# Attention scores in 48 drained stays of one and a half fills, in place of 63 stays of four or seven heads

## The chip, the cores and the metric

The kernel runs on one core of one Trainium2 chip. The metric is the device time of one execution in microseconds (us); a kernel's figure is the median of its runs. TensorE (PE) multiplies matrices into PSUM, a memory of eight banks of 128 partitions x 512 fp32 values; ScalarE (ACT) and VectorE (DVE) read PSUM, GpSimd (POOL) works on SBUF alone, and SyncE (SP) issues transfers.

## The reference

A gated mix of two branches over one sequence of 2048 tokens of width 512, in bf16:

```python
g = _sigmoid((x * gate_w).sum(-1, keepdims=True))
a = _A_ref(x, A_wq, A_wk, A_wv, A_wo, A_beta)     # attention with a memory, 32 heads of 16
b = _B_ref(x, B_W_gate, B_W_up, B_W_down)         # relu(x Wg) * (x Wu) Wd, inner width 1792
return g * a + (1 - g) * b
```

Branch A cuts the sequence into four segments of 512 tokens. In a segment each head has causal softmax attention over the segment alone, and it recalls from a running memory of the segments before:

```python
logits = jnp.einsum('bhqd,bhkd->bhqk', qs, ks) * scale + mask
p = _softmax(logits, axis=-1)
a_dot = jnp.einsum('bhqk,bhkd->bhqd', p, vs)
num = jnp.einsum('bhld,bhde->bhle', pq, M)
den = jnp.einsum('bhld,bhd->bhl', pq, z)[..., None] + 1e-06
o = g * a_mem + (1.0 - g) * a_dot
```

The step that the change touches is the first of these: the scores q k^T and their exponentials.

## The kernel before

**Plan and order.** The body doesn't issue instructions as it goes. `plan.add` (line 144) makes a numbered task with its engine, a modelled duration, what it depends on, and the PSUM banks and ring buffers that it takes (`need`) and gives back (`frees`). `ORDER` (line 31) is a list, written out, of all 1362 task numbers; `UNITS` (line 97) names the bank or buffer of each slot. `Plan.run` walks the list, and the tasks are emitted in that order, so that each engine's queue is a subsequence of it. The durations in the tasks play no part in what is emitted.

**TensorE's three ways of work.** A full product (`full`, line 491) uses the array as one tile of 128 x 128 (line 493) or, where `Plan.run` has marked the stretch as a column stretch, as four column tiles of 128 x 32 that stream at the same time (line 497). The attention output P V (`pv`, line 757), the memory update (line 880) and the denominators (line 814) always use column tiles. The scores (`visit`, lines 673 to 716) use four row tiles of 32 x 128: row tile j holds head j of a group of four, since a head has 16 channels and two heads of a pair share 32 rows. So every visit to the scores is a change of the array's tiling on the way in and one on the way out. This text calls a visit a **stay**.

**Units and fills.** A unit u (16 of them, four to a segment) is a group of eight heads over one segment's 512 queries. Its scores come as four **fills** of 4 x 512 columns (row tile j fills one bank of 512), the causal pieces in `PIECES` packed so that each fill is full; the 64-wide diagonal pieces ("d") of two units together make a fifth fill in every second unit. That is 72 fills. `tape` strings their 4 x 72 items (unit, fill, row tile) together, and `SIZES` (line 987) cuts the tape into 63 stays: 51 of four items and 12 of seven. A stay of four takes four banks, each row tile one; a stay of seven takes seven, and lasts as long as two fills, since three of its row tiles do two items and one does one. One bank (`HOST`, line 988) then belongs to a tile of the down projection that is open across the stay (`hosts`).

**After the scores.** One ACT instruction (line 714) takes the exponential of up to four banks at once, from PSUM into a bf16 tile `E` (six of them, `RE`), or `Em` for the diagonal. POOL masks the diagonal blocks of `E` (line 730), DVE those of `Em` (line 738). `pv` multiplies with V; DVE normalises and transposes (lines 788 to 769). Between the stays, PE runs the projections of q, k, v, the gate and up products of branch B (`ffn_tasks`, line 915) and the down and output products (`out_tile`, line 942), whose results DVE and ACT move out of PSUM bank by bank.

Of the kernel before, what the change touches and what calls it, by code (L numbers as in the profile page):

```python
# [12 lines left out]
P = 128  # L13
# [12 lines left out]
RE = 6  # L26
# [68 lines left out]
"""  # L95

UNITS = (
    "530476210000046222023013110375010151700000200100000010110000010010300002100011030239202431"
    "38122a1100320531063217203d01220031013b102c010200022111230020111123201232201323103121342013"
    "000000000230010000023000000000130003000005010027c60293205511810373200120410212106326a012d1"  # L100
    "1132232204b0001020011712110631071222222010322117021132520310000000003200000000320010000002"
    "3000300003200162687116300c222a31340019020b302321156037102132427150110d01020002317312117110"
    "31131346511047603102000000000720100000013000000000230100000050103234617c0128512d1031321522"
    "0010190103301a6136504b4077322200120110020"
)


class Slot:


    def __init__(self, cands):
        self.cands, self.units, self.left = tuple(cands), (), 0

# [79 lines left out]
def kernel(  # L193
# [56 lines left out]
    hT = ring([P, L], BF16, "hT", RH)  # L250
    T = ring([P, 2, L], F32, "T", 1)
    ex1 = ring([P, L], BF16, "ex1", 3)
    ktr = ring([P, L], BF16, "ktr", 4)
    pkT = ring([P, L], BF16, "pkT", 4)
    rgr = ring([P, L], BF16, "rgr", 3)
    och = ring([P, L], BF16, "och", 2)
# [816 lines left out]
```

## Time and profile before

| What | us |
|---|---|
| three runs, median (range) | 262.33 (262.08 to 262.55) |
| the profiled execution: its time | 262.61 |
| its span in the trace | 260.9 |
| DVE busy | 202.1 (77%) |
| ACT busy | 183.0 (70%) |
| POOL busy | 67.3 (26%) |
| PE weight loads busy | 120.7 (46%) |

A row of a timeline gives the start and the length of some instructions of one line that follow each other, in us from the span's start, then the engine, the line, the operation, output and inputs, the shape (rows x columns of the array tile, then the output) and the count. PE is a matrix multiplication, PEld a weight load. The length of a matmul in the trace includes its way through the array, so that matmuls overlap; what a matmul costs is read from one start to the next. A row of a group of instructions ends with busy time, mean ns of one, and the engine's idle time before them with what ended it.

### The profile page before, as it was taken

How to read it: one execution, taken by the hardware profiler on the slowest of the kernel's cores; microseconds unless marked ns; L12 is line 12 of the kernel's file. 1: busy time of each engine (PE TensorE's matmuls, PEld its weight loads, DVE VectorE, ACT ScalarE, POOL GpSimd, SP SyncE). 2: the span in 40 equal slices, each digit the busy share in tenths (PEclk: the TensorE clock that was granted, in tenths of full speed). 3: DMA queues.
4: the chain of work that ended last, by engine and by line, in shares of the span. 5: the costliest groups of instructions: out<-in, count | busy, mean ns of one | idle time of the engine just before them, and what ended most of it. 6: DMA issues, size and time to landing. Idle time of an engine off the chain costs nothing.

```text
span 260.9 us, 9058 instructions
## 1 busy us (share of the span) xinstructions
PE 254.1 (97%) x3914; PEld 120.7 (46%) x3942; DVE 202.1 (77%) x452; ACT 183.0 (70%) x186; POOL 67.3 (26%) x188
## 2 busy tenths in 40 slices
PE   8999999999999999999999999999999999999995
PEld 3444444444545444454545444444545444445445
DVE  2499889999888957998998894697888736596622
ACT  3199899998889678797377837989477875793000
POOL 8018742224322213113021242124112422112000
PEclk9999999999999999999999999999999999999999
DMA  7999963030006243300016541000000043000011
GB/s 194 314 284 259 283 140 105 3 68 13 3 23 132 64 114 75 68 3 3 15 35 107 167 110 57 4 0 8 14 0 10 7 145 112 0 3 3 3 40 43
DMA packets 31600, 19.75 MB, mean 76 GB/s; under 512 B 16072, under 2 KB 30024, under 8 KB 31560
## 3 DMA queue, kind: packets, MB, share of 16 engines
q1 hardware_dynamic: 31144, 18.90, 28.6%
q8 instruction: 31, 0.51, 0.9%
q10 hardware_dynamic: 416, 0.26, 0.3%
q14 instruction: 9, 0.07, 0.1%
HBM read 13.21 MB, written 2.55 MB: 60 GB/s over the span
## 4 chain that ended last, share of the span: by engine, by line
PE 97%; issue 1%; DVE 0%
PE ps L493 53%; PE ps L497 25%; PE ps L685 9%; PE ps L757 7%; PE ps L1006 1%; PE ps L880 1%; PE ps L855 0%; PE ps L531 0%; PE ps L814 0%; DVE osr L961 0%; PE ps L540 0%
## 5 line engine op out<-in xcount | busy, mean ns | idle before, releaser
L714 ACT ACTIVATE E<-ps 128x2048 bf16<-128x2048 f32 (+3 forms) x79 | 120.4, 1552 | 26.4 <-PE ps L685 25.6
L730 POOL TENSOR_SCALAR_AFFINE_SELECT E<-E 128x256 bf16<-128x256 bf16 x128 | 53.7, 448 | 155.0 <-ACT E L714 149.1
L931 DVE TENSOR_TENSOR hT<-ps,rgr 128x512 bf16<-128x512 f32 x56 | 37.8, 681 | 21.9 <-PE ps L493 13.5
L925 ACT ACTIVATE rgr<-ps 128x512 bf16<-128x512 f32 x56 | 32.7, 596 | 20.3 <-PE ps L493 11.1
L493 PE MATMUL ps<-xT,wu_sb 128*128 128x512 bf16 x158 | 41.9, 380 | 0.6 <-issue 0.5
L493 PE MATMUL ps<-xT,wg_sb 128*128 128x512 bf16 x132 | 34.9, 379 | 0.6 <-issue 0.3
L493 PE MATMUL ps<-wd_sb,hT 128*128 128x512 bf16 (+2 forms) x147 | 29.5, 339 | 1.4 <-issue 1.3
L685 PE MATMUL ps<-QT,KT 32*128 32x64 bf16 (+3 forms) x768 | 27.8, 244 | 0.0
L788 DVE STREAM_TRANSPOSE T<-ps 128x512 f32<-128x512 f32 x32 | 21.9, 701 | 3.5 <-PE ps L757 3.1
L497 PE MATMUL ps<-wd_sb,hT 128*32 128x512 bf16 x384 | 24.0, 380 | 0.0
L493 PEld LDWEIGHTS <-wu_sb 128*128 128x128 bf16 x164 | 14.9, 98 | 18.5 <-issue 2.5
L497 PE MATMUL ps<-xT,wg_sb 128*32 128x512 bf16 x344 | 23.1, 380 | 0.0
L685 PEld LDWEIGHTS <-KT 32*128 32x128 bf16 x768 | 11.0, 92 | 24.1 <-issue 22.8
L961 DVE TENSOR_SCALAR osr<-ps,ngcol 128x512 bf16<-128x512 f32 (+2 forms) x18 | 12.2, 682 | 11.3 <-PE ps L493 10.4
L493 PEld LDWEIGHTS <-wg_sb 128*128 128x128 bf16 x138 | 12.9, 98 | 15.7 <-issue 1.3
L493 PEld LDWEIGHTS <-hT 128*128 128x128 bf16 x156 | 13.5, 98 | 14.1 <-issue 2.3
L757 PE MATMUL ps<-E,Vp 128*17 128x320 bf16 (+3 forms) x512 | 19.1, 273 | 0.0
L714 ACT ACTIVATE Em<-ps 128x2048 bf16<-128x2048 f32 (+2 forms) x11 | 15.6, 1415 | 4.3 <-PE ps L685 4.1
L497 PE MATMUL ps<-xT,wu_sb 128*32 128x512 bf16 x240 | 16.2, 379 | 0.0
L588 DVE CAST QT<-ps 128x512 bf16<-128x512 f32 x16 | 10.9, 684 | 6.0 <-PE ps L493 5.5
L493 PE MATMUL ps<-xT,wq_sb 128*128 128x512 bf16 x49 | 14.3, 407 | 0.2 <-issue 0.2
L493 PE MATMUL ps<-wv_sb,xT 128*128 128x512 bf16 x54 | 13.9, 379 | 0.4 <-issue 0.3
(100 smaller groups left out, 308.7 us busy)
## 6 DMA issues: line engine op xcount, KB each, us to landing
out_dram<-osr SPq DMA_DIRECT2D x15, 128.0 KB
xn<-in_A_x_dram SPq DMA_DIRECT2D x3, 512.0 KB
xn<-coefs SPq DMA_DIRECT2D x6, 256.0 KB
cdr<-coefs SPq DMA_DIRECT2D x6, 256.0 KB
wg_sb<-in_B_W_gate_dram SPq DMA_DIRECT2D x2, 512.0 KB
wu_sb<-in_B_W_up_dram SPq DMA_DIRECT2D x2, 512.0 KB
wd_sb<-in_B_W_down_dram SPq DMA_DIRECT2D x2, 512.0 KB
wg_sb<-in_B_W_gate_dram SPq DMA_DIRECT2D x2, 384.0 KB
```

The costliest lines, as they stand in the source:

```text
L493: nc.tensor.matmul(out, lhsT=lhsT, rhs=rhs, start=start, stop=stop)
L497: nc.tensor.matmul(out[r], lhsT=lhsT[:, r], rhs=rhs, start=start, stop=stop, tile_position=(0, 32 * j))
L588: prj["q", seg, c] = plan.add("DVE", 600, key - RQK, lambda: nc.vector.tensor_copy(QT[i][:], bank(sl)), [a] + war, DVL, frees=[sl])
L685: nc.tensor.matmul(ps[:, o:o + w], lhsT=lhsT.rearrange("p h q -> p (h q)"), rhs=rhs, start=True, stop=True, tile_position=(32 * j, 0))
L714: lambda n0=n0, n1=n1, u=u, f=f, j0=j0, j1=j1: nc.scalar.activation(target(u, f, j0, j1), ps[:, banks[n0] * L:(banks[n0] + n1 - n0) * L], ...
L730: nc.gpsimd.affine_select(out=m[:, :, o:o + HP], in_=m[:, :, o:o + HP], compare_op=ALU.is_ge, fill=0.0, base=HP, pattern=[[0, 4], [1, HP]] ...
L757: nc.tensor.matmul(bank(sl)[32 * m:32 * m + HW, q:q + w], lhsT=(Vp[i] if n < 4 else Vm)[:, kb, r, 4 * c + j, 0:HW], rhs=rhs, start=(n == 0 ...
L788: done.append(plan.add("DVE", 633, key - RL, lambda r=r, sl=sl: nc.vector.transpose(T[ts.i][:, r], bank(sl)), [a] + done, 75 if r else 0, ...
L880: nc.tensor.matmul(bank(sl)[32 * j:32 * j + 32, 34 * g:34 * g + 34], lhsT=pK[i][:, t, g * P + 32 * j:g * P + 32 * j + 32], rhs=Vp[i][:, t, ...
L925: r = plan.add("ACT", 478, key - RL, lambda sl=gsl, rs=rs: nc.scalar.activation(rgr[rs.i][:], bank(sl), ACT.Relu), [g], ACL, frees=[gsl])
L931: nc.vector.tensor_tensor(hT[hs1.i][:], bank(sl), rgr[rs.i][:], ALU.mult)),
L961: nc.vector.tensor_scalar(osr[os.i][:, n0 - c0:n1 - c0], bank(sl)[:, 0:n1 - n0], ngcol[:, tt:tt + 1], None, ALU.mult)),
```

## The change

The tape of items goes. Each unit has three stays (48 in all), and each does one whole fill and half of another: fill 0 with the first half of fill 1, fill 2 with the other half of fill 1, fill 3 with the unit's own half of the diagonal fill. A stay takes three pairs of banks: the whole fill has a bank for each row tile, as before, and the half fill puts row tiles 0 and 1 into one bank and 2 and 3 into another, 256 columns each. So that two row tiles never write one bank at the same time, the stay has two parts with `nc.tensor.drain()` between them: in the first, row tiles 0 and 2 write their half fill and 1 and 3 the first 256 columns of their whole fill; in the second come the other 512 columns of each row tile. Exponentials go by bank pair, 1024 columns an instruction, three for each stay. The score matmuls become 928 from 768, since pieces are cut at column 256.

With it: a seventh `E` tile, `ktr` and `pkT` rings of three for four; each of the two `pv` groups of a unit waits for the masks of its own two fills alone; the diagonal mask goes by unit; the down projection's tiles take any free bank; `ORDER` and `UNITS` are new lists of 1401 tasks and 635 slots.

```diff
-RE = 6
+RE = 7
 ORDER = """
...
-    ktr = ring([P, L], BF16, "ktr", 4)
-    pkT = ring([P, L], BF16, "pkT", 4)
+    ktr = ring([P, L], BF16, "ktr", 3)
+    pkT = ring([P, L], BF16, "pkT", 3)
...
+    def pieces(u, f, c0, c1):
+
         if f == "d":
+            for kb in range(4):
+                yield kb, 2, kb * P, HP, HP * kb
+            return
+        for kb, q, o in PIECES[f // 2]:
+            a, b = max(o, c0), min(o + L - q, c1)
+            if a < b:
+                yield kb, 3 * (f % 2), q + a - o, b - a, a
+
+    def parts(u):
+
+        return [((u, 0, None), (u, 1, 0)), ((u, 2, None), (u, 1, 1)), ((u, 3, None), (u, "d", u % 2))]
+
+    def visit(u, n, key):
+        whole, half = parts(u)[n]
+        pairs = [(0, 1), (2, 3), (4, 5), (6, 7), (1, 2), (3, 4), (5, 6)]
+        sls = [Slot([(("ps", a), ("ps", b)) for a, b in pairs[k:] + pairs[:k]]) for k in range(3)]
+        h0 = 0 if half[1] == "d" else half[2] * L // 2
+        mm = ([], [])
+        for j in range(4):
+            n = 0
+            for part, c0, c1, late in (((half, h0, h0 + L // 2, 0), (whole, 0, L, 1)),
+                                       ((whole, 0, L // 2, 0), (whole, L // 2, L, 1),
+                                        (half, h0, h0 + L // 2, 1)))[j % 2]:
+                for kb, o, q, w, at in pieces(*part[:2], c0, c1):
+                    base = (2, j * L // 2 + at - h0) if part is half else (j // 2, j % 2 * L + at)
+                    mm[late].append((n, j, base, kb, o, q, w))
+                    n += w + 6
 
         def pe():
...
+            for late in range(2):
+                if late:
+                    nc.tensor.drain()
+                for _, j, (k, at), kb, o, q, w in sorted(mm[late]):
+                    rows = slice(32 * j, 32 * j + 32)
+                    at += sls[k].i * L
+                    nc.tensor.matmul(ps[:, at:at + w],
+                                     lhsT=KT[u % RK][rows, kb, o:o + 2].rearrange("p h q -> p (h q)"),
+                                     rhs=QT[u % RQ][rows, q:q + w],
+                                     start=True, stop=True, tile_position=(32 * j, 0))
...
+            def ex(k=k, f=f, h=h, sl=sl):
+                src = ps[:, sl.i * L:(sl.i + 2) * L]
+                if f == "d":
+                    dst = Em[:, :, h].rearrange("p j k q -> p j (k q)")
+                else:
+                    dst = E[(NFILL * u + f) % RE].rearrange("p (j q) -> p j q", j=4)
+                    dst = dst[:, 2 * k:2 * k + 2] if h is None else dst[:, :, h * L // 2:(h + 1) * L // 2]
+                nc.scalar.activation(dst, src.rearrange("p (j q) -> p j q", j=2 if h is None else 4),
+                                     ACT.Exp, scale=SCALE)
...
-        while any((u, f) not in tape_done for f in FILLS(u)):
-            score()
+        for n in range(3):
+            visit(u, n, KA(u - LEAD, AUNIT * n / 3))
...
-            a = plan.add("PE", 550, key - PVP + r, pv, masks + [prj["v", seg, t] for t in range(4)]
+            a = plan.add("PE", 550, key - PVP + r, pv, masks[r::2] + more + [prj["v", seg, t] for t in range(4)]
...
-            eread[NFILL * u + f] = [a]
+            eread[NFILL * u + f] = [groups[f % 2][1]]
...
-            sl = plan.one("ps", [HOST] if tt < 12 else OBANKS if n0 < 3 * P else (5, 4))
+            sl = work() if tt < NT - 1 else plan.one("ps", OBANKS if n0 < 3 * P else (5, 4))
```

More of the change, by code (lines that the diff above doesn't have):

```diff
@@ L31 @@
 ORDER = """
[63 rows of a table removed]
[65 rows of a table added]
 """
 UNITS = (
[L98 to L104, printed above, removed]
+    "731620540000016010041027222153010120600100100134000001011001250010010010000100110000000016"
+    "70007129322c70335135412b40472232214120362134021a4208117d0010223170512031222032012100100231"
+    "22355330612465120302300100164000111044000030110000000000200030000040111000151150016025b110"
+    "8102a0110021d71130217300202347151405c32097112110250001010020050012212001115304121451712030"
+    "00444000050100000000001601100000000011010100000000021011401d1107100a1175001112020173021901"
+    "70120600147168021c001b02100110007201204001726236055011437203210000000005000100000044402000"
+    "0000000003100100000000050011310102100154120511485027020b1172021d01392003120a223c7176411062"
+    "11001"
 )
@@ L572, in proj_q @@
         old = u - RQ
-        war = [att.get(("score", old)), att.get(("score", old // 2 * 2, "d"))]
+        war = [att.get(("score", old))]
         pwar = [att.get(("recall", old)), att.get(("denpe", old // 4, old % 4 // 2))]
@@ L600, in proj_k @@
         old = u - RK
-        war = [att.get(("score", old)), att.get(("score", old // 2 * 2, "d"))]
+        war = [att.get(("score", old))]
         a = matmuls(key, [(w, 0.25) for w in war if w], sl, proj_mm(wk_sb, c, seg),
@@ L651 @@
     PIECES = [[(0, HP, 0), (3, 7 * HP, 7 * HP)], [(1, 3 * HP, 0), (2, 5 * HP, 5 * HP)]]
-    eread, exps = {}, {}
-    def item(u, f, j):
-        rows = slice(32 * j, 32 * j + 32)
+    eread, exps, stays = {}, {}, []
+    def pieces(u, f, c0, c1):
         if f == "d":
-            for v in range(2):
-                i = (u + v) % RQ
-                for kb in range(4):
-                    yield (KT[(u + v) % RK][rows, kb, 2:4], QT[i][rows, kb * P:kb * P + HP],
-                           4 * HP * v + HP * kb, HP)
-        else:
-            i, r = u % RQ, f % 2
-            for kb, q, o in PIECES[f // 2]:
-                yield KT[u % RK][rows, kb, 3 * r:3 * r + 2], QT[i][rows, q:L], o, L - q
@@ L668, in target @@
-    def target(u, f, j0, j1):
-        if f == "d":
-            return Em[:, j0:j1].rearrange("p j v k q -> p (j v k q)")
-        return E[(NFILL * u + f) % RE][:, j0 * L:j1 * L]
-    def visit(items, key, banks):
-        mm, busy, fin = [], [0.0] * 4, []
-        for n, (u, f, j) in enumerate(items):
-            for lhsT, rhs, o, w in item(u, f, j):
-                mm.append((busy[j], j, n, lhsT, rhs, banks[n] * L + o, w))
-                busy[j] += w + 6
-            fin.append(busy[j])
-        mm.sort(key=lambda m: m[:3])
-        def pe():
-            for _, j, _, lhsT, rhs, o, w in mm:
-                nc.tensor.matmul(ps[:, o:o + w], lhsT=lhsT.rearrange("p h q -> p (h q)"), rhs=rhs,
-                                 start=True, stop=True, tile_position=(32 * j, 0))
-        runs = []
-        for n, (u, f, j) in enumerate(items):
-            if (runs and runs[-1][1:3] == [u, f] and runs[-1][4] == j and n - runs[-1][0] < CUT
-                    and banks[n] == banks[n - 1] + 1):
-                runs[-1][4:6] = j + 1, n + 1
-            else:
-                runs.append([n, u, f, j, j + 1, n + 1])
-        sls = [Slot([tuple(("ps", b) for b in banks[n0:n1])]) for n0, _, _, _, _, n1 in runs]
-        deps = []
-        for u, f in dict.fromkeys(it[:2] for it in items):
-            for w in ((u, u + 1) if f == "d" else (u,)):
-                deps += [prj["q", w // 4, w % 4]] + prj["k", w // 4, w % 4]
-        a = plan.add("PE", max(busy) / 2.4 + 17, key - QKP, pe, deps, 275, mode="row", need=sls, size=16)
-        if len(items) > 4:
-            before, after = hosts.pop(0)
-            a.deps.append((before, 0.0))
-            after.deps.append((a, 0.0))
-        for (n0, u, f, j0, j1, n1), sl in zip(runs, sls):
@@ new lines, in pieces @@
+            for kb in range(4):
[22 more added lines that the diff above has]
+                    n += w + 6
+        def pe():
+            for late in range(2):
[8 more added lines that the diff above has]
+                                     start=True, stop=True, tile_position=(32 * j, 0))
+        a = plan.add("PE", 1.5 * L / 2.4 + PELAG, key - QKP, pe,
+                     [prj["q", u // 4, u % 4]] + prj["k", u // 4, u % 4], 275, mode="row",
+                     need=sls, size=16)
+        if stays:
+            a.deps.append((stays[-1], 0.0))
+        stays.append(a)
+        att["score", u] = a
+        for k, sl in enumerate(sls):
+            f, h = (whole, half)[k // 2][1:]
@@ L705, in visit @@
             if f == "d":
-                att["score", u, "d"] = a
-                wars = [att[k] for k in (("pv", u - 1), ("pv", u - 2)) if k in att]
+                wars = [att.get(("pv", u - 2))]
             else:
                 wars = eread.get(NFILL * u + f - RE, [])
-                att["score", u] = a
-            rd = max(fin[n0:n1]) / 2.4 + 17
+            def ex(k=k, f=f, h=h, sl=sl):
[7 more added lines that the diff above has]
+                                     ACT.Exp, scale=SCALE)
@@ L712, in visit @@
             exps.setdefault((u, f), []).append(plan.add(
-                "ACT", 66 + (n1 - n0) * L / 1.2, key,
-                lambda n0=n0, n1=n1, u=u, f=f, j0=j0, j1=j1: nc.scalar.activation(
-                    target(u, f, j0, j1), ps[:, banks[n0] * L:(banks[n0] + n1 - n0) * L], ACT.Exp,
-                    scale=SCALE), [(a, 275 - max(0.0, max(busy) / 2.4 + 17 - rd))] + wars, ACL, frees=[sl]))
+                "ACT", 66 + 2 * L / 1.2, key, ex, [a] + wars, ACL, frees=[sl]))
     def attention(seg, c):
@@ L734, in attention @@
                                   lock=True))
-        if c % 2 == 0:
-            for v in range(2):
-                att["diag", u + v] = plan.add(
-                    "DVE", 605, KA(u - LEAD, AUNIT * 0.75), lambda v=v: nc.vector.tensor_tensor(
-                        Em[:, :, v], Em[:, :, v], tri[:, None, None, :].to_broadcast([P, 4, 4, HP]),
-                        ALU.min), exps[u, "d"], DVL, lock=True)
-        masks += [att["diag", u]] + att["vm", seg]
+        att["diag", u] = plan.add(
+            "DVE", 605, KA(u - LEAD, AUNIT * 0.75), lambda: nc.vector.tensor_tensor(
+                Em[:, :, u % 2], Em[:, :, u % 2], tri[:, None, None, :].to_broadcast([P, 4, 4, HP]),
+                ALU.min), exps[u, "d"], DVL, lock=True)
+        more = [att["diag", u]] + att["vm", seg]
         key = KA(u - LEAD, AUNIT * 0.7)
@@ L946, in out_tile @@
             w = n1 - n0
-            sl = plan.one("ps", [HOST] if tt < 12 else OBANKS if n0 < 3 * P else (5, 4))
-            prev, mine = None, []
+            sl = work() if tt < NT - 1 else plan.one("ps", OBANKS if n0 < 3 * P else (5, 4))
+            prev = None
             for f0, f1 in ((0, 5), (5, 10), (10, 14)):
@@ L955, in out_tile @@
                 prev.frees += tuple(h[1] for h in hs[f0:f1])
-                mine.append(prev)
             a = matmuls(key, got_o + [att["ot", 4 * seg + c] for c in range(NC)], sl, [
@@ L963, in out_tile @@
                 [a, att["ng", seg]] + b, DVL, need=[] if b else [os], frees=[sl]))
-            if tt < 12:
-                first = mine[0].deps[-1][0].deps[-1][0]
-                hosts.append((first, a))
         ffn["o", seg, tt % 4] = a
@@ L971, in out_tile @@
             1400 if tt == NT - 1 else 2400, frees=[os], xfer=400.0)
-    def FILLS(u):
-        return [0, 1, 2, 3] + ["d"] * (u % 2 == 0)
-    tape = [(u, f, j) for u in range(4 * NSEG) for f in FILLS(u) for j in range(4)]
-    tape_done, seen = set(), [0, 0]
-    def score():
-        v, n = seen
-        items = tape[n:n + SIZES[v]]
-        seen[:] = v + 1, n + len(items)
-        visit(items, KA(items[0][0] - LEAD, AUNIT * (n % 18) / 18), BANKS[v])
-        tape_done.update(it[:2] for it in items if it[2] == 3)
-    CUT = 4
-    SIZES = [4] * 18 + [4, 4, 7, 4, 7, 4, 7, 4, 7, 4, 4, 4, 4, 4, 4] * 3
-    HOST = 7
-    BANKS, at = [], 0
-    for n in SIZES:
-        few, many = iter(range(3)), iter(range(3, HOST))
-        BANKS.append([next(many if n > 4 and k // 4 * 4 >= at and k // 4 * 4 + 4 <= at + n and (
-            at % 4 or k < at + 4) else few) if n > 4 else k - at for k in range(at, at + n)])
-        at += n
-    hosts = []
+    PELAG = 100
     OTW, OBANKS, MEMGAP = 3, (7, 6), 1600.25
```

128 rows, old and new, of the table ORDER are left out of this document.

## The prediction

> **What bounds the kernel now.** I read the page's totals and slices first, then PE's waits, since the chain of waits lies on PE for nearly all of the span.
>
> ```profile
> span 260.9 us, 9058 instructions
> PE 254.1 (97%) x3914; PEld 120.7 (46%) x3942; DVE 202.1 (77%) x452; ACT 183.0 (70%) x186; POOL 67.3 (26%) x188
> ...
> PEclk9999999999999999999999999999999999999999
> ...
> PE 97%; issue 1%; DVE 0%
> ```
>
> ```profile
> PE ps L493 <- issue: 2.5, 16, 0.2
> PE ps L1006 <- PEq L1057: 0.8, 1, 0.8
> ```
>
> In all 260.9 us PE waits for no other engine after its first instruction: its list of waits has the start (0.8) and 16 short gaps of "issue", 2.5 in all, and no semaphore. The clock is full throughout. The end of PE's queue sets the time, so the change is worth what it adds to or takes from PE's own stream, as long as the new order keeps PE fed. Busy time doesn't show that stream (matmuls overlap, and a gap under 0.15 isn't counted as idle), so I went to PE's timeline around the stays.
>
> ```profile
> 66.53 0.40 PE L685 MATMUL ps<-QT,KT 32*128 32x448 bf16 x8
> 66.86 0.29 PE L814 MATMUL ps<-pqT,zbd 128*32 128x128 bf16 x8
> ...
> 68.17 1.04 PE L497 MATMUL ps<-wd_sb,hT 128*32 128x512 bf16 x16
> 69.14 0.61 PE L685 MATMUL ps<-QT,KT 32*128 32x320 bf16 x14
> ...
> 73.03 0.41 PE L685 MATMUL ps<-QT,KT 32*128 32x64 bf16 x26
> 73.37 1.04 PE L493 MATMUL ps<-wd_sb,hT 128*128 128x512 bf16 x4
> ...
> 76.72 0.63 PE L685 MATMUL ps<-QT,KT 32*128 32x448 bf16 x20
> 77.28 1.26 PE L497 MATMUL ps<-wd_sb,hT 128*32 128x512 bf16 x20
> ```
>
> ```profile
> 93.61 1.03 PE L493 MATMUL ps<-wd_sb,hT 128*128 128x512 bf16 x4 [0.16 <-issue]
> 94.48 1.03 PE L493 MATMUL ps<-wo_sb,oT 128*128 128x512 bf16 x4
> ...
> 97.93 1.03 PE L493 MATMUL ps<-xT,wu_sb 128*128 128x512 bf16 x4
> 98.89 0.40 PE L685 MATMUL ps<-QT,KT 32*128 32x320 bf16 x8
> 99.22 0.61 PE L493 MATMUL ps<-xT,wg_sb 128*128 128x512 bf16 x2
> ```
>
> The reader is to see three prices here. **A column**: four products of 512 columns take 94.48 - 93.61 = 0.87 from start to start, 0.216 each; without its fixed few ns a stream of 512 columns is 0.213 (128 columns 0.053). **The way in**: the four products that start at 97.93 have streamed at 97.93 + 4 x 0.216 = 98.79, and the stay's first matmul starts at 98.89. From column tiles it is the same: 68.17 + 4 x 0.216 = 69.03, then 69.14. So a change of tiling costs 0.10. **Stay and way out**: from 98.89 to 99.22 is 0.33, of which 0.213 is streaming and 0.12 the stagger of the tiles and the change back; at 66.53 it is 0.33 too. A stay of four costs 0.10 + 0.33 = 0.43. A stay of seven, at 76.72, takes 0.56, with the way in 0.66.
>
> **What goes.** 51 stays of four and 12 of seven: 51 x 0.43 + 12 x 0.66 = 29.8 us of PE.
>
> **What comes, without the drain.** 48 stays of 768 columns: 1.5 x 0.213 = 0.32, with stagger and way out 0.44, with the way in 0.54. The cut at column 256 makes 58 score matmuls of a unit's 48; a stay of 26 matmuls takes 0.34 (73.03 to 73.37), one of 8 takes 0.33, so ten more cost under 0.01. 48 x 0.54 = 25.9. So much of the change is a gain: 25.9 - 29.8 = **-3.9 us**. It has two sources: 15 stays fewer save about 15 x 0.22 = 3.3 of ways in and out with their stagger, and the remainder is the array time that the seven-item stays left empty (eight places, seven used).
>
> Whether the other changes of tiling stay as they are can be counted in the two order lists, with the rule that marks column stretches: 133 changes before, 103 after, and 30 is what 15 stays have. The full-width products are as many as before (964, with the narrow ones at the end); more of them stand in column stretches now, at the same 0.216 (the 16 matmuls from 68.17 are four groups of four, streamed in 0.86).
>
> **The drain.** 48 of them are added, each between two parts of a stay, and what is queued behind it is everything on PE: the weight loads of the second part too. No drain stands in mid-stream in this trace, so its cost g, from the last column of the first part to the first column of the second, is bounded from rows. The nearest row is PE's own drain behind its last matmul, read against that matmul:
>
> ```profile
> 257.50 0.39 PE L493 MATMUL ps<-wd_sb,hT 128*128 128x128 bf16 x4
> 257.72 0.39 PE L493 MATMUL ps<-wo_sb,oT 128*128 128x128 bf16 x4
> ```
>
> ```profile
> L1068 PEldq DRAIN  x2: 13/684/1355, 256.8 to 260.5; - x2
> ```
>
> ```profile
> 258.12 0.03 issue
> 258.14 0.35 DVE osr L961
> ```
>
> Four matmuls from 257.50 to 257.72 give 0.055 each, so the last one starts at 257.72 + 3 x 0.055 = 257.885 and has streamed at 257.94. Its result frees DVE at 258.14, and the drain, which began at 256.8, ends 1.355 later, at 258.15: 0.21 after the last column. A drain thus lasts until the results are in PSUM, not until the columns are in the array.
>
> Then PE starts again from an empty queue. The nearest row of that is its start, behind a semaphore instruction of 51 ns:
>
> ```profile
> L1057 PEldq EVENT_SEMAPHORE  x1: 51/51/51, 0.7 to 0.7; - x1
> ```
>
> ```profile
> 0.84 2.82 PE L1006 MATMUL ps<-const-bfloat16-1.0 128*128 128x512 bf16 x7 [0.84 <-PEq L1057]
> ```
>
> 0.7 (0.65 to 0.75) + 0.05 leaves 0.04 to 0.14 until the first matmul at 0.84. I take 0.06, near the lower end, because those first matmuls run at a mean of 0.4 us a start, twice the later price, so this row shows a slow array. **g = 0.21 + 0.06 = 0.27**; upper end 0.21 + 0.14 = 0.35. From below: a 64-column score matmul is held to last 0.189, of which 0.027 is streaming:
>
> ```profile
> L685 PE MATMUL ps<-QT,KT 32*128 32x64 bf16 x384 | 11.4, 189 | 0.0
> ```
>
> So results need 0.16 to land, the least for a drain that waits for them. Below that lies the change of tiling, 0.10, which also holds back weight loads, and at the far end 0: a drain whose wait is hidden. A gain from the drain itself is excluded, since both parts run on one array in order.
>
> The Trainium skill, "PSUM — Partial Sum Buffer", section "Engine vs sequencer instructions", says that a drain waits for the engine to go fully idle. The end of this trace agrees (0.21 past the last column), and by it g is at least the 0.16 above.
>
> **The sum.** 48 x 0.27 = 13.0; 13.0 - 3.9 = **+9.1 us**. The profiled execution took 262.61 (span 260.9, 1.7 around it), so 271.7; the median 262.33 is 0.28 below it: **271.4**. The change breaks even at g = 3.9 / 48 = 0.08. With g from 0.16 to 0.35 the sum is +3.8 to +12.9: 266.1 to 275.2.
>
> **Costed at nothing, and what covers it.** ACT: a fill by pairs is two instructions for one.
>
> ```profile
> L714 ACT ACTIVATE E<-ps 128x2048 bf16<-128x2048 f32 x49 | 91.9, 1876 | 14.6 <-PE ps L685 13.9
> ...
> L714 ACT ACTIVATE E<-ps 128x1024 bf16<-128x1024 f32 x12 | 12.0, 1024 | 3.1 <-PE ps L685 3.1
> ```
>
> ```profile
> ACT E L714 <- PE ps L685: 25.6, 34, 2.9
> ```
>
> ```profile
> 15.20:61.00 45.80, 45.22 (x674) 20.25 (x678) 42.47 (x103) 42.71 (x42) 20.44 (x65) 1.00 0.64 147
> ```
>
> Two of 1.024 for one of 1.876 is 0.17 more a fill, 12.4 over 72 fills at most (some are split already), and ACT is busy 183.0 of 260.9 and waits for score matmuls 25.6 us in 34 places. The tight stage is the first quarter (15.2 to 61.0), where ACT (the fourth pair of figures) is busy 42.71 of 45.80: its 18 fills become 36 instructions, 36 x 1.024 - 18 x 1.876 = 3.1 more, 45.8. The stage itself grows by twelve drains and shrinks by the stays: 45.8 + 12 x 0.27 + 12 x 0.54 - 18 x 0.43 = 47.8. The cover is thin but holds, and it holds because of the drains. Diagonal masks, POOL's masks and the transposes keep their number; the rings of three make a k projection's DVE work wait longer for a transfer, and DVE has 59 us idle, with nothing on PE waiting for it now. The seventh E tile and the halved lists of waits for pv take waits from ACT and PE that PE doesn't show. All of these end at zero unless the cover goes, which is the third rival.
>
> **Rival 1: the drain is no dearer than a change of tiling** (g 0.08 to 0.16). For it: the array does empty itself at each of the 126 ways in and out, at 0.10. Against it: 258.15. Time at 0.10: 48 x 0.10 - 3.9 = +0.9, 263.2; up to 266.1. The Trainium skill, "TensorEngine Tiling (Array Packing)", section "Key Properties", says that a change of tiling mode drains the TensorE. This trace shows 0.10 for one, under the 0.16 for results to land, so such a drain is not the instruction's.
>
> **Rival 2: the drain is hidden, and the kernel is faster.** If the drain held back only what follows by order while the weights of the second part were loaded meanwhile, g would be the stagger alone, 0.02 to 0.03: 262.3 - 3.9 + 48 x 0.025 = 259.6. It decides below g = 0.08. For it: row tiles load their weights beside other tiles' streams inside a stay (26 matmuls in 0.34). Against it: the weight loads of a stay never start before the stream ahead has ended, even without a drain:
>
> ```profile
> 69.14 0.33 PEld L685 LDWEIGHTS <-KT 32*128 32x128 bf16 x14 [0.42 <-issue]
> ```
>
> This is also the case in which the change doesn't do what it says, a drain that orders nothing.
>
> **Rival 3: PE waits for banks.** A stay needs six of eight banks, so the last stay's three exponentials must be over before it: 3 x 1.02 plus two other ACT instructions of 0.6 are 4.3, against 47.8 / 12 = 4.0 from stay to stay in the first quarter. If both always stood between the exponentials, twelve stays would wait 0.3 each, 3.6: 275.0; with waits elsewhere, to 278. Against it: the 42.71 of ACT's busy time, less 18 x 1.876, leaves 8.9 for all else, 0.75 a stay, so 3.8 on average.
>
> **Chances and range.** Forecast (g 0.16 to 0.35, PE fed) 0.64; rival 1 0.15, of which half lies within 0.2% of before; rival 2 0.12; rival 3 0.09. A difference under 0.2% (0.5 us) can't be told from none here. Faster is rival 2, 0.12; same 0.07; slower 0.64 + 0.08 + 0.09 = 0.81. The range goes from 263.0, g = 0.10, to 275.2, the upper end of g: it leaves out rival 2, the cheapest part of rival 1 and what of rival 3 is beyond 275.2, two in ten. The forecast's own range is 266.1 to 275.2.
>
> **What would show it.** 48 drains of PE's queue inside the stream; in each stay a gap of 0.27 between the two bunches of score matmuls, and 0.10 + 0.44 + 0.27 = 0.81 from the end of the stretch ahead to the start of the next. PE still without semaphore waits, ACT's exponentials 144 at 1.02, DVE's counts unchanged. The forecast is wrong if the gap is under 0.10 or PE's waits name ACT with more than a microsecond in all.

## The result and the profile after

| | us |
|---|---|
| before, median (range) | 262.33 (262.08 to 262.55) |
| after, median of four runs (range) | 275.28 (274.0 to 275.63) |
| ratio, with its 95% interval | 1.0485 (1.0449 to 1.0521) |
| the profiled execution after: time, span | 275.02, 273.0 |

The change makes the kernel 4.9% slower. The first view is the page after, with the rows that answer to those of before:

```profile
span 273.0 us, 10230 instructions
PE 262.4 (96%) x4429; PEld 129.4 (47%) x4429; DVE 203.4 (74%) x452; ACT 186.8 (68%) x240; POOL 66.4 (24%) x188
...
PEclk9999999999999999999999999999999999999999
...
PE 96%; issue 2%; DVE 0%; ACT 0%
...
L720 ACT ACTIVATE E<-ps 128x1024 bf16<-128x1024 f32 x128 | 125.2, 1025 | 40.0 <-PE ps L695 37.3
```

The chain of waits is PE's own stream as before, at full clock, and ACT waits more for scores than it did (37.3 against 25.6). PE itself waited for this (engine and line, what it waited for: us in total, times, longest; "issue" stands for a halt with no releaser, one for which the profile shows nothing that PE waited for):

```profile
PE ps L985 <- PEq L1036: 0.8, 1, 0.8
PE ps L885 <- issue: 0.5, 1, 0.5
PE ps L500 <- issue: 0.5, 1, 0.5
PE ps L500 <- DVE mzacc L901: 0.4, 1, 0.4
```

There is no wait for ACT, one for DVE, and two halts without a releaser. The 12 us are in the stays: from the first weight load of a stay to that of the next stretch, 48 stays take 35.5 us in this trace, and the 63 before took 23.5. PE's timeline, then its weight loads, around one stay of the first kind (14 matmuls: 4 ahead of the drain, 10 behind it):

```profile
114.45 1.03 PE L496 MATMUL ps<-xT,wg_sb 128*128 128x512 bf16 x4
115.41 0.79 PE L695 MATMUL ps<-QT,KT 32*128 32x256 bf16 x14
116.13 1.05 PE L500 MATMUL ps<-xT,wu_sb 128*32 128x512 bf16 x16
```

```profile
114.24 0.75 PEld L496 LDWEIGHTS <-wg_sb 128*128 128x128 bf16 x4
115.41 0.10 PEld L695 LDWEIGHTS <-KT 32*128 32x128 bf16 x4 [0.42 <-issue]
115.79 0.21 PEld L695 LDWEIGHTS <-KT 32*128 32x128 bf16 x10 [0.28 <-issue]
116.13 0.55 PEld L500 LDWEIGHTS <-wu_sb 128*32 128x32 bf16 x16
```

The stretch ahead has streamed at 114.45 + 4 x 0.216 = 115.31; the way in takes 0.10; from 115.41 to the next stretch it is 0.72, and in the middle the weights of the second part come 0.38 behind those of the first. The first part streams 256 columns, 0.107, so **the drain leaves a gap of 0.27 in which nothing streams**. The matmul row covers this up, since it merges both parts and counts the way through the array as busy; the weight loads' row shows it. The drain instructions themselves (x count: shortest, median, longest in ns, first and last start):

```profile
L691 PEldq DRAIN  x48: 292/621/1688, 16.0 to 247.8; - x48
```

A drain's own length isn't its price. Its row begins while matmuls ahead of it still have to start: 1 to 22 of them start while the row runs. So it lasts up to 1.7 us, of which the stream loses 0.27. The drain of the stay above alone:

```profile
L691 PEldq DRAIN  x1: 1688/1688/1688, 114.0 to 114.0; - x1
```

By the trace's records it starts at 114.04, so it ends at 115.73: 0.21 after the last column of the first part (115.52), and the second part starts 0.06 after that end. It is the same in every stay: the drain ends 0.18 to 0.24 after the last column (median 0.21), PE starts again 0.06 later, and the whole gap is 0.24 to 0.30, 13.3 us over the 48.

### The profile page after: what moved, and what is told of

Its sections match the earlier page's. It is cut to its first block, busy times and chain, and to the rows that moved or that the text cites. A ratio compares the mean times of both kernels' runs of the same rounds, so it can differ in the third digit from the quotient of the medians.

```text
span 273.0 us, 10230 instructions
## 1 busy us (share of the span) xinstructions
PE 262.4 (96%) x4429; PEld 129.4 (47%) x4429; DVE 203.4 (74%) x452; ACT 186.8 (68%) x240; POOL 66.4 (24%) x188
## 4 chain that ended last, share of the span: by engine, by line
PE 96%; issue 2%; DVE 0%; ACT 0%
PE ps L496 43%; PE ps L500 33%; PE ps L695 11%; PE ps L762 7%; PE ps L985 1%; PE ps L885 1%; PE ps L860 0%; PE ps L819 0%; PE ps L534 0%; ACT xT L549 0%; DVE osr L965 0%; DVE mzacc L901 0%
## 5 line engine op out<-in xcount | busy, mean ns | idle before, releaser
L720 ACT ACTIVATE E<-ps 128x1024 bf16<-128x1024 f32 x128 | 125.2, 1025 | 40.0 <-PE ps L695 37.3
L695 PE MATMUL ps<-QT,KT 32*128 32x64 bf16 (+4 forms) x928 | 33.3, 231 | 5.4
L496 PE MATMUL ps<-xT,wu_sb 128*128 128x512 bf16 x128 | 33.8, 380 | 0.0
L695 PEld LDWEIGHTS <-KT 32*128 32x128 bf16 x928 | 18.0, 92 | 32.2 <-issue 31.2
L500 PE MATMUL ps<-wd_sb,hT 128*32 128x512 bf16 x412 | 27.2, 380 | 0.5 <-issue 0.5
L500 PE MATMUL ps<-xT,wu_sb 128*32 128x512 bf16 x384 | 26.1, 380 | 0.4 <-DVE mzacc L901 0.4
L496 PEld LDWEIGHTS <-hT 128*128 128x128 bf16 x149 | 12.8, 98 | 12.7 <-issue 1.1
L720 ACT ACTIVATE Em<-ps 128x1024 bf16<-128x1024 f32 x16 | 16.4, 1022 | 3.5 <-PE ps L695 3.5
L496 PEld LDWEIGHTS <-wu_sb 128*128 128x128 bf16 x128 | 11.7, 98 | 13.6
L500 PEld LDWEIGHTS <-hT 128*32 128x32 bf16 x412 | 10.1, 97 | 8.9 <-issue 1.0
L762 PEld LDWEIGHTS <-Vp 128*17 128x17 bf16 x512 | 9.9, 92 | 8.4 <-ACT E L720 0.4
```

The lines of the kernel that those rows point to most:

```text
L496: nc.tensor.matmul(out, lhsT=lhsT, rhs=rhs, start=start, stop=stop)
L500: nc.tensor.matmul(out[r], lhsT=lhsT[:, r], rhs=rhs, start=start, stop=stop, tile_position=(0, 32 * j))
L695: nc.tensor.matmul(ps[:, at:at + w], lhsT=KT[u % RK][rows, kb, o:o + 2].rearrange("p h q -> p (h q)"), rhs=QT[u % RQ][rows, q:q + w], star ...
L720: nc.scalar.activation(dst, src.rearrange("p (j q) -> p j q", j=2 if h is None else 4), ACT.Exp, scale=SCALE)
L762: nc.tensor.matmul(bank(sl)[32 * m:32 * m + HW, q:q + w], lhsT=(Vp[i] if n < 4 else Vm)[:, kb, r, 4 * c + j, 0:HW], rhs=rhs, start=(n == 0 ...
```

## The experiments

### The drains taken out

```diff
             for late in range(2):
-                if late:
-                    nc.tensor.drain()
...
-                    base = (2, j * L // 2 + at - h0) if part is half else (j // 2, j % 2 * L + at)
+                    base = ((j // 2, L + at - h0) if j % 2 else (2, j * L // 2 + at - h0)) if part is half else (j // 2, j % 2 * L + at)
...
+                src = src.rearrange("p (j q) -> p j q", j=2 if h is None else 4)
+                if h is not None:
+                    src = src.rearrange("p (k j) q -> p k j q", j=2)[:, :, 0:1, :].to_broadcast([P, 2, 2, L // 2])
+                    dst = dst.rearrange("p (k j) q -> p k j q", j=2)
```

> The changed kernel with the drains left out, and with it what makes them needed: the half fill of row tiles 1 and 3 goes into their own banks (over columns they have written), so that no bank has two writers, and the exponential of the half fill reads the columns of row tiles 0 and 2 twice. Same matmuls, columns, exponentials and order; the scores of half of the heads in the half fills are left out. Theory (the 48 gaps of 0.277 us, 13.3 in all, lie bare on PE's stream): the gaps go, the stays lose their second stagger, and the time falls by 13 to 14, to 261 to 262.5. Rival (banks: with twelve drains fewer in the first quarter the stays come closer together than three exponentials): PE gets waits for ACT instead, and the time falls by less, to 264 or more, with ACT named in PE's waits.

Measured: 261.86 (260.82 to 263.98, ten runs), against 261.97 of the kernel before on the same chip: ratio 0.9999 (0.9972 to 1.0026). Between this and the changed kernel lie 0.0486 of 262, 12.7 us, for 48 drains. The same stay as above, in this kernel's PE timeline:

```profile
109.81 0.81 PE L496 MATMUL ps<-xT,wg_sb 128*128 128x512 bf16 x3
110.55 0.51 PE L693 MATMUL ps<-QT,KT 32*128 32x256 bf16 x14
110.99 1.05 PE L500 MATMUL ps<-xT,wu_sb 128*32 128x512 bf16 x16
```

From 110.55 to 110.99 is 0.44, where the drained stay took 0.72: 0.28 less. Its waits:

```profile
PE ps L496 <- issue: 1.3, 8, 0.2
PE ps L987 <- PEq L1038: 0.8, 1, 0.8
PE ps L887 <- issue: 0.8, 1, 0.8
PE ps L821 <- issue: 0.7, 1, 0.7
PE ps L764 <- DVE hT L938: 0.2, 1, 0.2
PE ps L500 <- DVE hT L938: 0.2, 1, 0.2
```

ACT is not among them, even with the stays 0.28 closer together. So the six banks of a stay and the exponentials by pairs don't hold PE up, and without the drains the slowdown is gone. The run also shows the other half of the sum: with the drains away, 48 stays are worth nothing measurable against 63, where 3.9 was reckoned. The two long halts in the list (0.7 and 0.8) are these:

```profile
60.57 0.23 PE L821 MATMUL ps<-pqT,zbd 128*32 128x128 bf16 x4
61.49 0.24 PE L821 MATMUL ps<-pqT,zbd 128*32 128x128 bf16 x4 [0.69 <-issue]
...
115.24 0.41 PE L887 MATMUL ps<-Vp,pK 128*32 128x34 bf16 x34
116.42 0.75 PE L887 MATMUL ps<-Vp,pK 128*32 128x34 bf16 x30 [0.76 <-issue]
```

### A second drain behind the first

```diff
                 if late:
                     nc.tensor.drain()
+                    nc.tensor.drain()
```

> The changed kernel with two drains, one behind the other, in each stay. Theory (a drain is a wait for results to land, 0.21, and a restart of 0.06): the second drain finds the engine idle and costs its own execution and little else, under 0.06 each, 0 to 3 in all: 275 to 278.5. Rival (a drain has a fixed price of 0.27 whatever is in flight): 48 x 0.27 = 13 more, 288.

Measured: 278.74 (278.53 to 278.81), ratio 1.0647 (1.0631 to 1.0662). That is more than one drain by 3.5 with the medians, 0.07 each, and by 4.2 with the ratios, 0.09 each. PE's timeline of the same stay, where the gap is now wide enough to be shown as idle:

```profile
116.11 1.03 PE L496 MATMUL ps<-xT,wg_sb 128*128 128x512 bf16 x4
117.07 0.29 PE L696 MATMUL ps<-QT,KT 32*128 32x256 bf16 x4
117.53 0.40 PE L696 MATMUL ps<-QT,KT 32*128 32x448 bf16 x10 [0.17 <-issue]
117.86 1.05 PE L500 MATMUL ps<-xT,wu_sb 128*32 128x512 bf16 x16
```

```profile
L692 PEldq DRAIN  x48: 13/13/13, 16.9 to 252.3; - x48
```

117.07 to 117.86 is 0.79 by these rows; by the records, before rounding, this stay takes 0.08 more than with one drain. The second drain finds the engine idle and lasts 13 ns, yet costs 80: that much comes with a drain even when nothing is in flight, and the remaining 0.19 or so of the first one's price only where results are. The rival's 288 is out. The theory had the second drain at under 0.06, which was too little, and its upper end, 278.5, was 0.2 too low.

### A change of tiling in the place of the drain

```diff
                 if late:
-                    nc.tensor.drain()
+                    nc.tensor.matmul(ps[:, sls[0].i * L:sls[0].i * L + HP], lhsT=ident[:], rhs=ident[:, 0:HP],
+                                     start=True, stop=True)
```

> As the kernel without drains (the half fill of row tiles 1 and 3 goes over their own banks), with one full-array matmul of 64 columns in the place of each drain, so that the array changes its tiling twice between the two parts of a stay. Theory (a change of tiling costs 0.10, less than the drain, since it doesn't wait for results to land): 2 x 0.10 + 0.03 = 0.22 to 0.23 in place of 0.277, 48 times, 2.5 less than the changed kernel: 272.5. Rival (a change of tiling in mid-stay empties the array as a drain does, 0.27 each): 288.

Measured: 273.16 (272.17 to 273.73), ratio 1.0431 (1.0401 to 1.0461). The same stay:

```profile
113.33 1.03 PE L496 MATMUL ps<-xT,wg_sb 128*128 128x512 bf16 x4
114.29 0.29 PE L696 MATMUL ps<-QT,KT 32*128 32x256 bf16 x4
114.51 0.20 PE L691 MATMUL ps<-ident 128*128 128x64 bf16 x1
114.64 0.40 PE L696 MATMUL ps<-QT,KT 32*128 32x448 bf16 x10
114.97 0.40 PE L500 MATMUL ps<-xT,wu_sb 128*32 128x512 bf16 x4
```

From 114.29 + 0.107 = 114.40 to 114.51 the array changes to one tile (0.11), 64 columns take 0.03, and at 114.64 it has changed back (0.10). The two changes and the 64 columns between them cost 0.24, less than the 0.27 of one drain. The stay takes 0.68 against 0.72. Over the kernel without drains the time is 0.0432 of 262 more, 11.3 us, 0.235 for each of 48. The rival is out. The theory's 272.5 was 0.7 too low, and by the times alone the gain over the drain is not clear: the intervals of the two ratios overlap (1.0461 and 1.0449 are the ends). What shows it is the trace.

### A drain where the array changes its tiling anyway

The kernel before, with a drain at the head of each of its 63 stays:

```diff
         def pe():
+            nc.tensor.drain()
             for _, j, _, lhsT, rhs, o, w in mm:
```

> The kernel before with a drain at the head of each of its 63 stays, where the array changes its tiling anyway. Theory (drain and change of tiling wait for the same array, so the longer of the two counts): 0.27 in place of 0.10, 63 times, 10.7 more: 273. Rival a (they add): 63 x 0.27 = 17 more, 279.4. Rival b (the change of tiling covers the drain): 262.3, no change.

Measured: 272.65 (272.56 to 273.05) against 261.97, ratio 1.0418 (1.0403 to 1.0434): 10.7 more, as the theory had it. PE's timeline at the stay that the prediction read at 98.89:

```profile
101.62 1.03 PE L493 MATMUL ps<-xT,wu_sb 128*128 128x512 bf16 x4
102.75 0.40 PE L686 MATMUL ps<-QT,KT 32*128 32x320 bf16 x8
103.08 0.60 PE L493 MATMUL ps<-xT,wg_sb 128*128 128x512 bf16 x2
```

101.62 + 4 x 0.216 = 102.48, and the stay starts at 102.75: a way in of 0.27 in place of 0.10, and the same 0.33 to the next stretch. Drain and change of tiling don't add; the longer counts here.

### The halts without a releaser

The two halts of the changed kernel stand in the middle of a batch of column tiles (PE's timeline):

```profile
62.21 0.60 PE L500 MATMUL ps<-wd_sb,hT 128*32 128x512 bf16 x7
63.31 0.39 PE L500 MATMUL ps<-wd_sb,hT 128*32 128x512 bf16 x1 [0.50 <-issue]
...
120.67 0.35 PE L885 MATMUL ps<-Vp,pK 128*32 128x34 bf16 x28
121.54 0.52 PE L885 MATMUL ps<-Vp,pK 128*32 128x34 bf16 x36 [0.52 <-issue]
```

Seven of eight column matmuls run, and the eighth comes late (0.50 of idle, 0.66 counted from the end of the seven's streams), though it belongs to the same product as the three ahead of it; nothing that it reads can be late for it alone. Two kernels shift everything in PE's program:

```diff
-            nc.tensor.matmul(bank(warm[k])[:, 0:w], lhsT=one.to_broadcast([P, P]),
-                             rhs=one.to_broadcast([P, w]), start=True, stop=True)
+            for c in range(0, w, 64):
+                nc.tensor.matmul(bank(warm[k])[:, c:c + 64], lhsT=one.to_broadcast([P, P]),
+                                 rhs=one.to_broadcast([P, 64]), start=True, stop=True)
```

> The changed kernel with its seven warm-up matmuls at the start cut into 50 of 64 columns: the same columns, 43 matmuls and 43 weight loads more ahead of everything else, so that all that follows stands 86 instructions further on in PE's program. Asked is what the long halts of PE inside a column stretch are (0.66 at 63.3 and 0.69 at 121.5 in the changed kernel, with no semaphore in their rows). Theory (they hang on the place in PE's instruction stream, which is brought in by transfers of 16 KB): they move 43 matmuls towards the start of the program, the first from one matmul ahead of the first denominators to about 44 ahead. Rival (they wait for a result or a transfer of data): they stay at the same matmul. The time is that of the changed kernel within 1 us.

> As the last, with the warm-up in 100 matmuls of 32 columns, 186 instructions more. Theory: the halts stand 93 matmuls earlier in the program than in the changed kernel, or at other block ends, or the transfer is in time there and they are gone. Rival: the same matmuls as in the changed kernel. The time is that of the changed kernel within 1 us; if 32 columns cost more than 27 ns each at the start, up to 1 us more.

Measured: 274.85 (274.46 to 275.45) and 274.64 (274.43 to 275.61), ratios 1.0506 (1.0481 to 1.053) and 1.0497 (1.0472 to 1.0523): the changed kernel's time. Both halts are gone from their places; each kernel has one elsewhere. With 86 instructions more:

```profile
34.76 0.20 PE L762 MATMUL ps<-Em,Vm 128*17 128x64 bf16 x3
35.51 0.28 PE L762 MATMUL ps<-Em,Vm 128*17 128x64 bf16 x13 [0.55 <-issue]
```

With 186 more:

```profile
145.96 0.39 PE L500 MATMUL ps<-wd_sb,hT 128*32 128x512 bf16 x4
147.21 1.70 PE L500 MATMUL ps<-wd_sb,hT 128*32 128x512 bf16 x28 [0.86 <-issue]
```

The rival (a late result or a transfer of data) would have left them at the same matmul, and falls. The theory foresaw them 43 and 93 matmuls earlier, and they aren't there either; only the last clause of the second expectation held (other places, or gone). So the halts follow the place of an instruction in PE's program and not what the instruction reads.

The traces say which places. Count PE's instructions from the start, two for each weight load (itself and its matmul) and one for each drain or semaphore instruction: ahead of the halt stand 1729 in the changed kernel, 705 with 86 more and 5058 with 186 more. These lie 4 x 256 and 13 x 256 apart, to one instruction. The kernel without drains and the one with a change of tiling have a halt behind 1730, where other matmuls stand than in the changed kernel. PE's program comes in transfers of 16 KB (queue: transfers, MB, share of the DMA engines):

```profile
q8 instruction: 35, 0.57, 0.9%
```

These are 35 for 8914 recorded instructions, 255 for each. In all five halts PE goes on 1.3 to 1.5 us after such a transfer has landed. So these halts stand where one block of instructions ends and the next begins; a block that comes too late for PE fits all of them, as the theory had it. What remains open is why a block is late at one such place and not at the others, and what the second halts are: the changed kernel's at 121.54 (behind 3721) and the one at 116.42 without drains (behind 3710) are not at the end of a block, though they too end 1.0 to 1.4 us after a transfer.

## Why the prediction was right, and where it was off

**Direction and main term: right.** The prediction took g = 0.27 from the drain at the end of the trace before (0.21 past the last column) and from PE's start (0.06). In the changed kernel the gap of the stay shown is 0.27, from drained to undrained stay it is 0.72 - 0.44 = 0.28, and the kernel without drains is 12.7 us away from the changed one, against 48 x 0.27 = 13.0. The split held too: 0.21 from the last column to the drain's end and 0.06 to PE's next start, in the trace after. The second drain's 0.08 is another thing than this 0.06, and the prediction had no use for it.

**The time: low.** 271.4 was forecast, 275.28 measured, 0.1 above the range's upper end of 275.2 (the ratio times 262.33 is 275.05, 0.1 below it). That it comes out so near this end is luck and no merit of the range: the end stands for a gap of 0.35 a drain, and the gap was 0.27. The width kept for one term covered an error in another. The term that failed is the gain of -3.9:

| term | forecast | measured |
|---|---|---|
| 48 drains | +13.0 | +12.7 (ratio of the changed kernel less ratio without drains); +13.3 by the gaps in the trace |
| 48 stays for 63, without drains | -3.9 | 0.0 (-0.7 to +0.7) |

The stay itself was well read: way in 0.10, then 0.44, both as reckoned; with 0.10 + 0.44 + 0.27 = 0.81 forecast for a drained stay and 0.10 + 0.72 = 0.82 seen. What failed is the step "costed at nothing": that PE would stay as fed as before. The new order has halts that the old one has not. By the lists of waits (which leave out the first 0.15 of each) there are 1.5 us in two places without drains and 1.0 in two with them, and 0.4 for DVE in both.

Counted from the end of the columns to the next start, they make up most of the loss. The profiled spans are 260.3 without drains and 260.9 before, 0.6 less where 3.9 was forecast, so 3.3 are missing. The trace without drains has halts of 0.85, 0.94 and 0.24 (the two shown above, the second in two pieces), two that are too short for the list (0.29 inside a stay, 0.21 in a batch of column tiles), and 0.30 and 0.22 for DVE: 3.05 in all. The trace before has none of these. A likely reason stands in the prediction itself, where more products stand in column stretches now, "at the same 0.216": their columns cost the same, but a product takes four matmuls and four weight loads there in place of one, and PE has 4429 weight loads for 3942, 12% more instructions in the same time. That this is why blocks of instructions come late in the new order and not in the old is not tested.

One execution is not the median: the ten runs of the kernel without drains lie 3.2 apart, three times as far as those of the kernel before (261.53 to 262.56).

**Rival 1, a drain as cheap as a change of tiling: wrong.** 0.27 against 0.10, in one trace. The Trainium skill, "TensorEngine Tiling (Array Packing)", section "Key Properties", has a change of tiling drain the engine. The runs show that this is another thing than the instruction: with a drain ahead of the change the way in is 0.27, without one 0.10.

**Rival 2, a hidden drain: wrong.** The weight loads of the second part start 0.27 after the first part has streamed.

**Rival 3, waits for banks: wrong.** PE's waits name ACT neither with the drains nor without. The cover that the prediction called thin held without the drains too.

**The count of the stalls before.** The prediction took 16 gaps of "issue", 2.5 us, for gaps. The page before has 3914 matmuls to 3942 weight loads, and the page after 4429 of each and none of those short gaps. The kernel without drains has 4405 to 4429, and eight such gaps (the 1.3 in its list of waits, which are not among the halts above). So they are matmuls without a record. Nothing hung on it, but "PE never waits" was truer than the row said.

## What to carry to other kernels

A TensorE drain in mid-stream costs 0.27 us here, 0.21 until it ends and 0.06 until PE starts again, and it pays only where it saves more than that: here 48 of them (13 us) were to buy 15 stays' ways in and out, 0.2 each (3 us), and halts of the new order took even these. Where two parts of a row-tiled batch must be kept apart, a change to another tiling and back takes a little less of the stream, 0.24 with a 64-column matmul, and by an estimate from these rows (0.11 and 0.10) 0.21 if useful work stands between; no kernel here orders shared banks in that way. Before an edit at a saturated engine, price the instruction from the one place where the old trace has it, even if that is the kernel's end.

## What the runs showed that was not expected

- A drain's row is 292 to 1688 ns long, with 1 to 22 matmuls ahead still to start, and its price is 0.24 to 0.30 throughout; a drain behind a drain lasts 13 ns and costs about 80.
- PE halts for 0.5 to 0.9 us by the lists of waits in the middle of a batch, with no semaphore, at places that move when instructions are added ahead. Five of the halts stand at the ends of blocks of 256 instructions and end 1.3 to 1.5 us after a transfer of instructions has landed; two others don't stand there. Together they cost 1.0 to 2.5 us in a trace.
- Fifteen stays fewer, with 30 changes of tiling fewer, gave no time that could be measured: 0.9999 (0.9972 to 1.0026). The stays themselves were shorter, and halts in the new order took most of the gain.
